# Pairing the last rows of the first two batches in a token-mixing matmul, and moving one transpose and one set of loads

## The chip, the core and the metric

The kernel runs on one core of a Trainium2 chip. The metric is the time of one execution on the device in microseconds (us), the median of several runs; lower is better. The engines are the tensor engine (PE in the profile; PEld is its weight load), the vector engine (DVE), the scalar engine (ACT), GpSimd (POOL) and the sync engine, whose queue (SPq) issues most transfers. PE's results go to PSUM, which this kernel divides into a pool of four single banks ("big") and one of two double banks ("sm").

## The reference, cut to what matters

Eight batches of 576 rows go through linear attention and then through an MLP mixer:

```python
# attention, per batch and head (8 heads of 64 columns)
q_p, k_p = phi(q), phi(k)                   # phi(x) = elu(x) + 1
x = (q_p @ (k_p.T @ v)) / (q_p @ k_p.sum(0) + 1e-6)   # 576 x 512 once the heads are joined
# mixer, per batch
h  = np.maximum(x.T @ w_tok1, 0) @ w_tok2   # mixes the 576 rows, through 256 features
u  = x + h.T
out = u + np.maximum(u @ w_ch1, 0) @ w_ch2  # mixes the 512 columns, through 1536 features
```

576 rows are four blocks of 128 and 64 rows over. The kernel treats two batches as a pair: the 64 last rows of both stand in one tile `ut` of 128 rows (even batch in rows 0 to 63, odd batch in rows 64 to 127). So the transposes and channel matmuls of the last rows are done once per pair.

## The kernel before: the parts that the change and the argument touch

`mm1` and `mm2` are the token matmuls, `mm3` and `mm4` the channel matmuls. `utr` transposes `u` into `uT` for `mm3`, and `utr_tail` transposes `ut` into `uTt`. For pair 0 these transposes are done on PE, later by transfers. `mm2_tails` handles the last rows of both batches together, for pairs 1 to 3 only:

```python
def mm2_tails(p):
    ps = ps_sm.tile([128, 2, DM], FP32, name="h_ps", tag="sm")[:, 0]
    for kt in range(NT):                       # NT = 2
        at = D * (T * kt + 2 * R)
        for b in range(2):                     # both halves of the array, 64 columns each
            nc.tensor.matmul(out=ps[half[b]], lhsT=w2p[:, at:at + D], rhs=ar[b][:, kt, :],
                             start=(kt == 0), stop=(kt == NT - 1))
    for b in range(2):
        h = half[b]
        nc.vector.tensor_tensor(out=ut[p % 2][h], in0=ps[h], in1=x[b][h, R], op=ALU.add)
```

In pair 0, batch 0's last rows are done alone, early, and batch 1's alone, later, with a full-width matmul of which half is thrown away:

```python
def mm2_first_tail():                          # batch 0, between the third and fourth mm3 group
    ps = sm_tile()[:, 0]
    for kt in range(NT):
        nc.tensor.matmul(out=ps[half[0]], lhsT=w2p[:, D * (T * kt + 2 * R):][:, 0:D],
                         rhs=ar[0][:, kt], start=(kt == 0), stop=(kt == NT - 1))
    nc.vector.tensor_tensor(out=ut[0][half[0]], in0=ps[half[0]], in1=x[0][half[0], R], op=ALU.add)

# ... the end of pair 0's first stage, and the start of batch 1's mm3
fill += [(23, fn) for fn in (
    lambda: mm4_end(0, 0), lambda: mm4_end(0, 1), lambda: mm2_half(1, 0),
    lambda: mm4_end(0, 2), lambda: mm2_half(1, 1), lambda: utr(1, [0]),
    lambda: mm2(1, [R]), lambda: utr(1, [1]), lambda: mm4_end(0, 3))]
run(big, sorted(fill, key=lambda e: e[0]))

for mc in range(3):
    mm3(1, mc, range(0, 2))                    # first halves of three groups, three banks of "big"
utr_tail(0)
big = [lambda mc=mc: mm3(1, mc, range(2, 4)) for mc in range(3)] + ...   # (cut)
```

A number such as `(23, fn)` says after which block of the big matmuls a piece is issued. `mm4_end(0, t)` is the DVE add that empties output block t of batch 0 out of its bank. Each engine gets its instructions in the order of the program, and a bank goes to the next user when its last reader is done.

Names in the profile lines below: `c_ps` is the bank of an `mm3` group (four matmuls for 128 of the 1536 features; the first three groups of batch 1 are split into halves of two), `h_ps` that of `mm2` or `mm4`, `tp` that of transposes. "kv" is the block of 72 small matmuls for `k_p.T @ v` of a batch. ACT and DVE share what stands between the matmuls: exp (tile `e`), relu (`cr`, `ar`), copies, and the "v cast", which turns v into bf16 for kv, one half on each of the two engines.

## Time and profile before

| | |
|---|---|
| time, median of 3 runs (range) | 263.65 us (263.41 to 263.68) |
| span in the profile | 261.8 us |
| PE busy; PE's share of the chain that ended last | 96%; 90% |
| DVE busy, ACT busy | 61%, 50% |
| granted PE clock | 1.000 |

PE is almost never idle, so the question for every piece is what it adds to PE's row of instructions or where it makes PE wait. The prediction below shows the lines. Starts in them are in us from the start of the span. A merged line gives the start, the length from the first start to the last end, and the count.

### The profile page before, as it was taken

What the parts mean: (1) busy time and instruction counts of PE and PEld (TensorE: products, weight loads), DVE (VectorE), ACT (ScalarE), POOL (GpSimd) and SP (SyncE); (2) the same over time, 40 slices, a digit from 0 to 9 for tenths busy, and PEclk for the clock granted to TensorE, in tenths of its full rate; (3) what the DMA queues carried; (4) which work ended last, traced back from release to release, by engine and by line L of the source; (5) the groups of instructions that cost most, each with busy time, mean ns of one, the idle gap of its engine ahead of it and who ended that gap; (6) DMA issues with size and microseconds to landing.
All of it is one profiled execution on the core that took longest, in us unless ns stands there. A gap on an engine that the chain in (4) does not pass through costs nothing.

```text
span 261.8 us, 5158 instructions
## 1 busy us (share of the span) xinstructions
PE 252.1 (96%) x2102; PEld 132.2 (50%) x2120; DVE 158.9 (61%) x313; ACT 130.9 (50%) x202; POOL 35.7 (14%) x58
## 2 busy tenths in 40 slices
PE   7799999999999999999999999999999999999993
PEld 3584455555744554455554554455554554444642
DVE  5865969966739687948674377939674263420122
ACT  4755773378374468336780468335780453026300
POOL 9760210110001300030001300030001300000000
PEclk9999999999999999999999999999999999999999
DMA  7999999699307994899999990770066500730043
GB/s 256 249 204 278 370 192 377 240 224 410 119 9 141 201 376 187 124 242 382 322 398 229 303 356 3 168 167 20 3 139 115 120 3 2 154 105 3 0 102 98
DMA packets 50087, 48.34 MB, mean 185 GB/s; under 512 B 30288, under 2 KB 35536, under 8 KB 50064
## 3 DMA queue, kind: packets, MB, share of 16 engines
q1 hardware_dynamic: 41904, 35.53, 46.9%
q0 software_dynamic: 7440, 11.44, 20.8%
q10 hardware_dynamic: 720, 1.05, 1.2%
q8 instruction: 16, 0.26, 0.4%
q14 instruction: 7, 0.06, 0.1%
HBM read 35.85 MB, written 9.44 MB: 173 GB/s over the span
## 4 chain that ended last, share of the span: by engine, by line
PE 90%; DMA 3%; ACT 2%; DVE 1%; POOL 1%; issue 1%; ACTq 0%; POOLq 0%
PE h_ps L529 33%; PE c_ps L503 32%; PE a_ps L248 5%; PE c_ps L517 4%; PE h_ps L261 4%; PE nd_ps L210 3%; DMA cr<-in_v_dram 3%; PE kv_ps L169 2%; PE h_ps L566 1%; PE bank L440 1%; POOL qT L610 1%; PE h_ps L282 1%; PE bank L405 1%; PE bank L378 0%; ACT u L303 0%
## 5 line engine op out<-in xcount | busy, mean ns | idle before, releaser
L503 PE MATMUL c_ps<-uT,wc 128*128 128x512 bf16 x384 | 91.4, 379 | 0.0
L510 ACT ACTIVATE cr<-c_ps 128x512 bf16<-128x512 f32 x91 | 53.4, 599 | 75.6 <-PE c_ps L503 75.5
L529 PE MATMUL h_ps<-wc,cr 128*128 128x512 bf16 x363 | 84.3, 379 | 0.5
L529 PEld LDWEIGHTS <-cr 128*128 128x128 bf16 x372 | 35.6, 98 | 41.7 <-issue 1.2
L503 PEld LDWEIGHTS <-wc 128*128 128x128 bf16 x384 | 35.7, 98 | 36.6 <-issue 1.2
L551 POOL DMA_DIRECT2D out_dram<-o_sb x24 | 14.5, 608 | 150.9 <-DVE o_sb L546 150.7
L546 DVE TENSOR_TENSOR o_sb<-h_ps,u 128x512 f32<-128x512 f32 x31 | 21.0, 687 | 21.0 <-PE h_ps L529 20.9
L222 DVE TENSOR_TENSOR x<-nd_ps,den 128x512 bf16<-128x512 f32 (+1 forms) x42 | 25.3, 602 | 1.4
L139 DVE TENSOR_SCALAR e<-e 128x1152 bf16<-128x1152 bf16 x30 | 14.0, 468 | 15.8 <-ACT e L125 15.7
L125 ACT ACTIVATE e<-q_raw 128x1152 bf16<-128x1152 f32 x16 | 18.5, 1160 | 5.7 <-DMA q_raw<-in_q_dram 5.5
L273 DVE TENSOR_TENSOR u<-h_ps,x 128x1024 bf16<-128x1024 f32 x12 | 14.3, 1219 | 10.1 <-PE h_ps L261 10.1
L125 ACT ACTIVATE e<-k_raw 128x1152 bf16<-128x1152 f32 x16 | 18.7, 1169 | 2.3 <-DMA k_raw<-in_k_dram 2.3
L219 DVE TENSOR_SCALAR den<-nd_ps 128x8 f32<-128x8 f32 (+1 forms) x42 | 6.8, 163 | 17.9 <-PE nd_ps L210 17.2
L210 PEld LDWEIGHTS <-qT 128*128 128x128 bf16 x140 | 11.4, 98 | 9.3 <-issue 0.2
L210 PE MATMUL nd_ps<-kvbd,qT 128*128 128x130 bf16 x140 | 15.1, 223 | 0.0
L248 PE MATMUL a_ps<-x,w 128*128 128x512 bf16 x50 | 13.9, 379 | 0.3
L556 DVE TENSOR_TENSOR o_sb<-h_ps,ut 128x512 f32<-128x512 f32 x4 | 2.8, 689 | 18.7 <-PE h_ps L529 18.7
L151 ACT CAST vs<-v_raw 128x1152 bf16<-128x1152 f32 x12 | 13.9, 1160 | 0.0
L251 ACT ACTIVATE ar<-a_ps 128x512 bf16<-128x512 f32 x14 | 7.6, 594 | 11.4 <-PE a_ps L248 11.4
L261 PE MATMUL h_ps<-ar,w2p 128*128 128x512 bf16 x48 | 12.5, 379 | 0.1
L140 DVE TENSOR_TENSOR qp<-e,y 128x1152 bf16<-128x1152 bf16 x16 | 12.1, 759 | 0.6
L131 DVE TENSOR_SCALAR y<-q_raw 128x1152 bf16<-128x1152 f32 x16 | 12.1, 757 | 0.3
(109 smaller groups left out, 221.3 us busy)
## 6 DMA issues: line engine op xcount, KB each, us to landing
k_raw<-in_k_dram SPq DMA_DIRECT2D x16, 576.0 KB, 9.1
q_raw<-in_q_dram SPq DMA_DIRECT2D x16, 576.0 KB, 7.0
v_raw<-in_v_dram SPq DMA_DIRECT2D x14, 576.0 KB, 10.8
out_dram<-o_sb POOLq DMA_DIRECT2D x24, 256.0 KB, 4.5
wc<-in_moe_w_ch_dram POOLq DMA_DIRECT2D x8, 384.0 KB, 9.5
out_dram<-o_sb SPq DMA_DIRECT2D x9, 128.0 KB, 2.3
out_dram<-o_sb ACTq DMA_DIRECT2D x7, 128.0 KB, 2.6
out_dram<-o_sb POOLq DMA_DIRECT2D x6, 128.0 KB, 7.1
```

The costliest lines, as they stand in the source:

```text
L125: nc.scalar.activation(out=e, in_=f, func=AF.Exp)
L139: nc.vector.tensor_scalar(out=e, in0=e, scalar1=1.0, scalar2=None, op0=ALU.min)
L210: nc.tensor.matmul(out=o[:, a], lhsT=qT[b][:, t0:t0 + 128], rhs=kvbd[b][:, c, a], start=True, stop=True)
L222: nc.vector.tensor_tensor(out=x[b][:, rs[0]:rs[0] + m, HG * D * g:HG * D * (g + 1)].rearrange("p r (h d) -> p r h d", h=HG), in0=v_[:, :, ...
L248: nc.tensor.matmul(out=ps[:, mt], lhsT=w1t[:, b, ms] if r == R else w1[:, r, ms], rhs=x[b][:, r, :], start=(r == 0), stop=(r == R))
L261: nc.tensor.matmul(out=ps[:, i], lhsT=w2v(kt, r, b), rhs=ar[b][:, kt, :], start=(kt == 0), stop=(kt == NT - 1 and not add))
L273: nc.vector.tensor_tensor(out=u[b][:, rs[0]:rs[0] + m], in0=ps[:, 0:m], in1=x[b][:, rs[0]:rs[0] + m], op=ALU.add)
L503: nc.tensor.matmul(out=ps, lhsT=wc1[:, kj, 128 * mc:128 * mc + 128], rhs=uT[b][:, :, kj], start=(kj == 0), stop=(kj == NDM - 1))
L510: nc.scalar.activation(out=cr[b][:, mc, :], in_=ps, func=AF.Relu)
L529: nc.tensor.matmul(out=ps, lhsT=crt[:, kc, :] if t == 8 else cr[b][:, kc, 128 * r:128 * r + 128], rhs=wc2[:, kc, :], start=(kc == 0), stop ...
L546: nc.vector.tensor_tensor(out=o, in0=ps, in1=u[b][:, r, :], op=ALU.add)
L551: (nc.scalar if last and e else put).dma_start(out=outv[2 * p + b, :, 2 * r0 + e:2 * r0 + e + 2 * m - 1:2], in_=live["o"][half[e], 0:m])
```

## The change

Its intent: the last rows of pair 0 are paired like those of the later pairs. Four matmuls in two places become four in one place that run two at a time, which saves time on PE. Their transpose moves behind the fourth matmul group of the next stage (group 3 in the code, which counts from zero), as `ut` is now ready later. The loads of batch 5 go behind pair 1's transpose of the last rows in the transfer queue.

```diff
     def mm2_tails(p):
-        ps = ps_sm.tile([128, 2, DM], FP32, name="h_ps", tag="sm")[:, 0]
+        ps = bank() if p == 0 else ps_sm.tile([128, 2, DM], FP32, name="h_ps", tag="sm")[:, 0]
...
-    def mm2_first_tail():                 # the whole function goes
...
-    fill = [(2, mm2_first_tail)]
+    fill = []
...
-        lambda: mm2(1, [R]), lambda: utr(1, [1]), lambda: mm4_end(0, 3))]
+        lambda: mm2_tails(0), lambda: utr(1, [1]), lambda: mm4_end(0, 3))]
...
     for mc in range(3):
         mm3(1, mc, range(0, 2))
-    utr_tail(0)
...
+    fill += [(3, lambda: utr_tail(0))]
...
             if n == 2:
-                fill += [(12 + d, lambda: load_all(5, "qkv"))]      # d = 1 here
+                fill += [(16, lambda: load_all(5, "qkv"))]          # pair 1's transpose is at 15
```

More of the change, by code (lines that the diff above doesn't have):

```diff
@@ L453, in mm2_first @@
                                 in1=x[0][:, rs[0]:rs[0] + 2, cs], op=ALU.add)
-    def mm2_first_tail():
-        ps = sm_tile()[:, 0]
-        for kt in range(NT):
-            nc.tensor.matmul(out=ps[half[0]], lhsT=w2p[:, D * (T * kt + 2 * R):][:, 0:D],
-                             rhs=ar[0][:, kt],
-                             start=(kt == 0), stop=(kt == NT - 1))
-        nc.vector.tensor_tensor(out=ut[0][half[0]], in0=ps[half[0]], in1=x[0][half[0], R],
-                                op=ALU.add)
     def utr_first(js, put):
```

## The prediction

> **What bounds the kernel now.** I read the page's engine table, its clock strip and the chain of work that ended last first, to see which engine sets the end.
>
> ```profile
> PE 252.1 (96%) x2102; PEld 132.2 (50%) x2120; DVE 158.9 (61%) x313; ACT 130.9 (50%) x202; POOL 35.7 (14%) x58
> ...
> PEclk9999999999999999999999999999999999999999
> ...
> PE 90%; DMA 3%; ACT 2%; DVE 1%; POOL 1%; issue 1%; ACTq 0%; POOLq 0%
> ```
>
> The tensor engine (PE) carries 90% of the chain, at full clock throughout. Only work taken out of its stream, or a gap in it, moves the end; the vector engine (DVE), the scalar engine (ACT) and the transfers count only where PE waits for them. So I went to the timeline of each place that the diff touches. The first is where the last rows of batch 0 are now done alone:
>
> ```profile
> 23.64 1.24 PE L503 MATMUL c_ps<-uT,wc 128*128 128x512 bf16 x5
> 24.81 0.62 PE L458 MATMUL bank<-ar,w2p 128*64 128x512 bf16 x2
> 25.36 0.82 PE L503 MATMUL c_ps<-uT,wc 128*128 128x512 bf16 x3
> ```
>
> Columns: start, length, engine, line, operation. To see here: a 512-column matmul lasts 0.38 us but the next starts 0.216 us after it (a run of 8 such spans 1.73 us in the chain). The last c_ps start is 23.64 + 1.24 - 0.38 = 24.50; the next c_ps is at 25.36. So the two 64-wide matmuls cost 25.36 - 24.50 - 0.216 = 0.64 us, not 2 x 0.216 = 0.43.
>
> The later pairs already use the paired form, four 64-wide matmuls:
>
> ```profile
> 103.99 1.89 PE L529 MATMUL h_ps<-wc,cr 128*128 128x512 bf16 x8
> 105.81 0.62 PE L282 MATMUL h_ps<-ar,w2p 128*64 128x512 bf16 x4
> 106.37 7.08 PE L529 MATMUL h_ps<-wc,cr 128*128 128x512 bf16 x31
> ```
>
> The same sum: 106.37 - (103.99 + 1.89 - 0.38) - 0.216 = 0.65 us for four. The four take what two take: each pair runs side by side.
>
> The third place is the changeover from pair 0's output to batch 1, on PE and then on DVE:
>
> ```profile
> 52.51 0.59 PE L261 MATMUL bank<-ar,w2p 128*128 128x512 bf16 x2
> 52.94 0.61 PE L316 MATMUL tp<-identity,u 128*128 128x128 bf16 x8
> 53.45 1.46 PE L503 MATMUL c_ps<-uT,wc 128*128 128x512 bf16 x6
> 54.74 0.39 PE L481 MATMUL tp<-identity,ut 128*128 128x128 bf16 x4
> 54.96 1.24 PE L503 MATMUL c_ps<-uT,wc 128*128 128x512 bf16 x5
> ```
>
> ```profile
> 52.70 0.69 DVE L320 COPY uT<-tp 128x1024 bf16<-128x1024 bf16 x1 [0.15 <-PE tp L316]
> 53.43 0.69 DVE L269 TENSOR_TENSOR ut<-bank,x 64x512 bf16<-64x512 f32 x1
> 54.15 0.69 DVE L546 TENSOR_TENSOR o_sb<-h_ps,u 128x512 f32<-128x512 f32 x1
> ```
>
> To see: PE is unbroken, and DVE works without a break from 52.70. Three matmul groups (six c_ps records) start between 53.45 and 54.53 while the fourth output block's bank is held until 54.84, when the last of these DVE adds ends. Four banks exist in this pool. So one of the three groups reuses the bank of the last rows. Freed at 53.43 + 0.69 = 54.12, it can only serve the third group, whose two matmuls start at about 54.31 and 54.53. Its slack is thus only about 0.2 us.
>
> The last place is the tail matmul of pair 1, with the wait in the DMA queue:
>
> ```profile
> 127.80 1.03 PE L261 MATMUL h_ps<-ar,w2p 128*128 128x512 bf16 x4
> 128.81 1.05 PE L517 MATMUL c_ps<-uTt,wc 128*128 128x128 bf16 x16
> ```
>
> ```profile
> 111.44 2.32 SPq L112 DMA_DIRECT2D q_raw<-in_q_dram  x2
> 113.85 1.81 SPq L112 DMA_DIRECT2D k_raw<-in_k_dram  x2
> 115.71 1.63 SPq L112 DMA_DIRECT2D v_raw<-in_v_dram  x2
> 117.47 3.62 SPq L492 DMA_TRANSPOSE uTt<-ut  x1
> 121.20 2.62 SPq L112 DMA_DIRECT2D q_raw<-in_q_dram  x2
> ```
>
> The transpose of the last rows stands behind six loads of batch 5 and takes 11.3 us to land (the maximum of its three in the view by tile; the median is 2.8), so at 128.8. Four matmuls from 127.80 should hand over at 128.66; the next starts at 128.81. PE loses 0.15 us there.
>
> **What the Trainium skill says.** "TensorE: Matmul & The Clock Gate", part 3 (The mechanism) says that matmuls on different tiles of the array run concurrently; the pair of 0.65 us above agrees. "TensorEngine Tiling (Array Packing)", Key Properties: "Changing tiling mode (not just tile) drains the TensorE". The trace agrees: 0.64 - 0.43 = 0.21 us is paid for going into the 64-wide form and back. Its section PSUM Bottleneck says that tiling speeds PE but not the emptying of PSUM; the trace agrees, as two 64-row adds (two DVE instructions, 1.39 us at 106.48) follow the paired form, one add of 0.69 us the single form. "DMA: Bandwidth & Descriptors", Issuing engines are not separate DMA queues, says all transfers interleave on 16 engines; moving the loads therefore moves no bytes, only their order.
>
> **The change part by part.**
>
> 1. The two 64-wide matmuls at 24.8 us go: -0.64 us of PE. One DVE add (0.68 us) goes too, in a stretch where DVE is near saturated (it does y, relu, min, max = 0.76 + 0.68 + 0.45 + 0.76 = 2.65 us per three groups, and PE needs 12 x 0.216 = 2.59). From here PE runs 0.64 us earlier, if batch 1's data are there. By the issue times and landing times of the transfers, its q block lands at about 18.54 + 12.0 = 30.5 us and is used at 31.23; 31.23 - 0.64 = 30.6, just enough. The second weight block of the channel output lands at about 36.9 and its matmuls start after the 37.2 to 38.0 kv block: about 0.4 us of room remain. Batch 2's q lands at 43.2 and holds ACT (idle 4.4 us), but ACT then waits 1.9 us more for PE, so nothing is lost. The shift should reach 52 us nearly whole.
> 2. At 52.5 us, two full-width matmuls (0.43 us) become four 64-wide ones (0.65): +0.22. Net PE work of 1 and 2: -0.42 us.
> 3. DVE gets a second add in the changeover: it is busy from 52.70 - 0.64 = 52.06; copy to 52.79, two adds to 52.79 + 1.39 = 54.18. The third group wants that bank at 54.31 - 0.42 = 53.89. It waits 0.33 us (with about 0.05 of handover). Of the 0.42 only 0.09 is left at this point.
> 4. The four transposes of the last rows (0.22 us at 54.74) leave this place and come back unchanged after the fourth matmul group of the stage: -0.22, then +0.22. Their ACT copy (0.59 us) moves from ahead of the relus to behind the fourth. ACT is continuously busy from 55.16 to 62.3, and PE waits about 0.16 us for it in this stretch (30 groups' matmuls take 6.63 us, not 30 x 0.216 = 6.47). The relus that free banks come relatively sooner in the new order, so I credit 0.10 us.
> 5. Loads of batch 5 behind the transpose: it then follows the qT transposes at 111.4 and lands by 115 or so, far ahead of 128.7: -0.15 us. The loads start about 1.5 us later (the other two transposes of this kind took 1.2 to 1.4 us to issue). Batch 5's q landed about 7.6 to 8.2 us after issue, 119 to 121, and is used from 123.1 (DVE) and 123.7 (ACT): no new wait.
>
> Sum: -0.09 (what is left of parts 1 to 3) - 0.10 - 0.15 = -0.34 us, 263.3 us.
>
> **The rivals.**
>
> - *Nothing waits.* The bank choice or DVE's order comes out kindlier; then -0.42 - 0.16 - 0.15 = -0.73, 262.9 us. For it: slack of a few tenths in most places. Against: DVE has no idle slot between 52.70 and 55.5.
> - *The early shift is eaten by transfers.* Batch 1's blocks land at fixed times, and DVE and ACT are fed by them 0.1 to 0.7 us after landing. If 0.3 us is lost there, DVE starts its adds later as well; together with the bank wait the changeover would come out 0.2 us later than before, leaving only the -0.15: 263.5 to 263.7 us. For it: q used at 31.23 just after landing. Against: no DMA wait is listed before ACT or DVE there.
> - *ACT becomes the bound after 55 us.* With the uTt copy behind the fourth relu, the fifth waits 0.59 us more. If PE then stalls for a bank, or kv waits for the v cast, +0.2 to +0.4 us: up to 263.8 us. For it: ACT's unbroken row. Against: the same copy stood before the first relu until now, so the sum of work is the same.
> - *The later loads starve batch 5.* If they land 3 us later, ACT would block with exp at 123.7, and relus behind it: +0.5 us or so. Against: some 2.5 us of room, and the queue is drained soon after either way.
>
> **Range and chances.** The terms lie between -0.75 and +0.3 us. The three runs before span 0.27 us, so a chip's scatter adds 0.1 to 0.15 on either side. Predicted 263.3 us; 8 times in 10 between 262.7 and 263.8. A change of 2% is 5.3 us, seven times the whole gain; only an unforeseen ordering trouble could reach it: faster 0.005, within 2% 0.985, slower 0.01.
>
> **What would show it.** In the changed kernel's timeline: no 64-wide matmuls at 24.8 and four near 52; kv at 37.2 earlier by about 0.6 (part 1). Two 64-row adds back to back on DVE near 52.8, and the third matmul group of batch 1 starting only after them (part 3): if it follows the second without a gap, that step is wrong and the time nearer 262.9. The handover at the next kv block (61.7 before) earlier by only 0.1 to 0.3 (part 4). The uTt transpose landing before 120 and no 0.15 us gap at its first use (part 5). A DMA wait before exp of batch 1 or 5 would speak for the second or fourth rival; a time above 264 us would mean that a term is missing.

## The result, and the profile after

| | before | changed |
|---|---|---|
| median of 4 runs | 263.66 us (263.41 to 263.92) | 263.41 us (263.19 to 264.26) |
| span in the profile | 261.8 us | 261.7 us |

The ratio is 0.9996, 95% interval 0.9972 to 1.002. Ratios here are the mean time of one kernel's fast runs over that of the other's fast runs of the same rounds, so not quite the ratio of the medians quoted. By the time alone the change cannot be told from nothing: one run of the changed kernel was 264.26 at a granted clock of 0.993. The trace can resolve more, because its steps agree between runs to a few hundredths of a microsecond.

One correction comes first. The start of the first large matmul depends on a load (v of batch 0) and differs from run to run: 21.50 in the trace of before, 21.76 in this one, and from 20.99 to 22.05 over all traces, whatever the kernel. I therefore count stretches from event to event and not from the span's start.

The changed kernel's PE rows from the first mm3 matmul to the first kv block, the stretch in which the two lone 64-wide matmuls stood:

```profile
21.76 1.02 PE L494 MATMUL c_ps<-uT,wc 128*128 128x512 bf16 x4
22.62 0.61 PE L460 MATMUL tp<-identity,u 128*128 128x128 bf16 x8
23.06 9.84 PE L494 MATMUL c_ps<-uT,wc 128*128 128x512 bf16 x44
...
36.79 0.78 PE L169 MATMUL kv_ps<-vs,kp 64*64 64x65 bf16 x72
```

The 44 matmuls from 23.06 now stand in one line, with no other matmul among them. The ends of the same stretch in the kernel before:

```profile
21.50 1.02 PE L503 MATMUL c_ps<-uT,wc 128*128 128x512 bf16 x4
...
37.19 0.78 PE L169 MATMUL kv_ps<-vs,kp 64*64 64x65 bf16 x72
```

From 21.76 to kv at 36.79 it is 15.03 us; before it was 37.19 - 21.50 = 15.69. So 0.66 us came out, where 0.64 had been forecast.

The changeover to batch 1, PE and then DVE, the counterpart of the lines from 52.51 on in the prediction:

```profile
52.19 0.62 PE L282 MATMUL bank<-ar,w2p 128*64 128x512 bf16 x4
52.75 0.62 PE L316 MATMUL tp<-identity,u 128*128 128x128 bf16 x8
53.21 3.89 PE L494 MATMUL c_ps<-uT,wc 128*128 128x512 bf16 x16
56.93 0.39 PE L472 MATMUL tp<-identity,ut 128*128 128x128 bf16 x4
57.15 4.48 PE L494 MATMUL c_ps<-uT,wc 128*128 128x512 bf16 x20
61.63 0.78 PE L169 MATMUL kv_ps<-vs,kp 64*64 64x65 bf16 x72
```

```profile
52.30 0.69 DVE L320 COPY uT<-tp 128x1024 bf16<-128x1024 bf16 x1 [0.15 <-PE tp L316]
52.91 1.38 DVE L286 TENSOR_TENSOR ut<-bank,x 64x512 bf16<-64x512 f32 x2
54.32 0.69 DVE L537 TENSOR_TENSOR o_sb<-h_ps,u 128x512 f32<-128x512 f32 x1
```

How to read a stall out of a merged line: 16 matmuls without a gap span 15 x 0.216 + 0.38 = 3.62 us, and the line says 3.89. So 0.27 us of waiting is inside it. The 20 matmuls from 57.15 span 19 x 0.216 + 0.38 = 4.48, so there is none. (The 44 above would span 9.67 and take 9.84: a wait of 0.17 us, which the kernel before has too, in the eight matmuls ahead of the lone ones.) In the chain of work that ended last, the piece that goes from DVE to PE names the place:

```profile
52.30 0.60 DVE uT L320
52.91 0.67 DVE ut L286
53.59 0.71 DVE ut L286
54.34 1.04 PE c_ps L494 x4
```

The two adds end at 52.91 + 1.38 = 54.29 and the third group starts at 54.34. Those two adds have become part of the chain; before, PE had no DVE step here. Behind the third group the chain leaves PE once more and runs over relu, exp and a v cast on ACT and DVE to the next kv block. What that costs is small and comes up under end_first_tail6.

From the transposes of batch 1's u (52.06 before, 51.66 now) to kv of batch 2 (61.68 before, 61.63 now) it was 9.62 us and is 9.97. Of the 0.66 us won, 0.35 is given back in this stretch. The lines of before:

```profile
52.06 0.61 PE L316 MATMUL tp<-identity,u 128*128 128x128 bf16 x8 [0.24 <-ACT u L303]
...
54.96 6.79 PE L503 MATMUL c_ps<-uT,wc 128*128 128x512 bf16 x30
61.68 0.78 PE L169 MATMUL kv_ps<-vs,kp 64*64 64x65 bf16 x72
```

The transfer queue and the first use of pair 1's `uTt`:

```profile
107.12 4.10 SPq L199 DMA_TRANSPOSE qT<-qp  x2
111.31 3.05 SPq L483 DMA_TRANSPOSE uTt<-ut  x1
114.46 1.05 SPq L112 DMA_DIRECT2D q_raw<-in_q_dram  x2
...
119.19 1.53 SPq L112 DMA_DIRECT2D q_raw<-in_q_dram  x2
```

```profile
127.84 1.03 PE L261 MATMUL h_ps<-ar,w2p 128*128 128x512 bf16 x4
128.70 1.06 PE L508 MATMUL c_ps<-uTt,wc 128*128 128x128 bf16 x16
```

The transpose is issued 6 us earlier. Its first use follows the four matmuls after 128.70 - 127.84 = 0.86 us = 4 x 0.216: no gap. Before it was 128.81 - 127.80 = 1.01.

### The profile page after: what moved, and what is told of

It reads as the page before. It is cut to its first block, busy times and chain, and to the rows that moved or that the text cites. A ratio compares the mean times of both kernels' runs of the same rounds, so it can differ in the third digit from the quotient of the medians.

```text
span 261.7 us, 5173 instructions
## 1 busy us (share of the span) xinstructions
PE 252.2 (96%) x2120; PEld 132.1 (50%) x2120; DVE 159.0 (61%) x313; ACT 130.7 (50%) x202; POOL 35.9 (14%) x58
## 4 chain that ended last, share of the span: by engine, by line
PE 88%; DVE 3%; DMA 3%; ACT 3%; POOL 1%; issue 1%; ACTq 0%; POOLq 0%
PE h_ps L520 33%; PE c_ps L494 29%; PE a_ps L248 6%; PE c_ps L508 4%; PE h_ps L261 4%; PE nd_ps L210 3%; DMA cr<-in_v_dram 3%; PE kv_ps L169 2%; PE h_ps L557 1%; PE bank L440 1%; ACT e L125 1%; POOL qT L601 1%; PE h_ps L282 1%; DVE kp L140 1%; DVE ut L286 1%
## 5 line engine op out<-in xcount | busy, mean ns | idle before, releaser
L251 ACT ACTIVATE ar<-a_ps 128x512 bf16<-128x512 f32 x14 | 7.6, 595 | 10.7 <-PE a_ps L248 10.7
```

## The experiments

All kernels gave correct results. One run of before, at 297.54 us and a clock of 0.853, is left out of the ratios.

Four stretches of the trace carry the reading. They are differences of two start times on PE:

* **A**: first mm3 matmul to kv of batch 1 (the lone matmuls stood here);
* **B**: transposes of batch 1's u to kv of batch 2 (the changeover);
* **C**: kv of batch 4 to the first matmul on pair 1's `uTt`;
* **tail**: the start of that matmul from the span's start.

| kernel | A | B | C | tail | median | before, same rounds | ratio (95%) |
|---|---|---|---|---|---|---|---|
| before (trace) | 15.69 | 9.62 | 14.57 | 128.81 | | | |
| changed: run change | 15.03 | 9.98 | 14.42 | 128.62 | 263.15 | 263.93 | 0.9974 (0.9946 to 1.0002) |
| changed: change_again | 15.03 | 9.97 | 14.42 | 128.36 | 263.42 | 263.64 | 0.9987 (0.9954 to 1.002) |
| loads_only | 15.69 | 9.62 | 14.42 | 128.68 | 263.81 | 263.93 | 1.0 (0.9973 to 1.0026) |
| pairs_only | 15.03 | 9.98 | 14.91 | 128.85 | 264.02 | 263.93 | 1.0 (0.998 to 1.002) |
| end_first | 15.04 | 9.70 | 14.48 | 128.15 | 262.99 | 263.93 | 0.9962 (0.9941 to 0.9982) |
| end_first_again | 15.16 | 9.71 | 14.41 | 127.72 | 262.92 | 263.64 | 0.9962 (0.9927 to 0.9997) |
| end_first_loads_back | 15.03 | 9.71 | 14.86 | 128.89 | 263.26 | 263.64 | 0.9982 (0.9945 to 1.0018) |
| end_first_tail6 | 15.27 | 9.63 | 14.42 | 127.75 | 262.91 | 263.95 | 0.9966 (0.9939 to 0.9993) |
| tail6_again | 15.03 | 9.63 | 14.54 | 127.89 | 263.10 | 263.64 | 0.9968 (0.9936 to 0.9999) |
| third_add | 15.15 | 10.71 | 14.42 | 129.22 | 264.01 | 263.95 | 1.0001 (0.9976 to 1.0026) |
| tail_old_place | 15.03 | 10.05 | 14.53 | 129.10 | 263.60 | 263.95 | 0.9987 (0.996 to 1.0014) |

C varies by about 0.1 us between traces even where nothing in it was touched (the first changed trace has 14.51), so only the 0.4 to 0.5 us steps in it and the gap at its end are used.

My theory: the matmuls come out as computed, and the third group of batch 1 then waits for DVE's second add, because it takes the bank of the last rows. The rivals: transfers that arrive at fixed times eat the gain in A; or ACT's row bounds the stretch B.

### change and change_again: the changed kernel once more

No edit.

> The changed kernel again, unaltered, to see its traced steps on another execution and its time beside the others of these rounds. Theory (the third matmul group of batch 1 waits for two vector adds): its start stands about 0.3 us late against an unbroken row of the groups before it, and the time is 0.1 to 0.5 us under the kernel before. Rival (the early gain is lost to transfers): no gap ahead of the third group, and the stretch from the first c_ps matmul to the kv block at 37 us is not shorter than before. The start of the first kv matmuls at 11 us is set by a load and may differ by 0.3 us from run to run in any kernel.

> The changed kernel once more, in the same rounds as the two reordered ones. Between 0.2 and 0.5 us under the kernel before by the traced steps; single runs spread by over 1 us, so the rounds may not resolve it.

A is shorter by 0.66 us in both, and the 0.27 us gap is in both: each has the 16 matmuls in 3.89 us. change_again is the cleanest pair with the trace of before, as both have their first mm3 matmul at 21.50. Its span is 261.3 us against 261.8, and the last block of matmuls starts at 254.63 against 255.09: 0.46 us earlier. That is 0.66 - 0.35 + 0.15. The times point the same way (ratios 0.9974 and 0.9987), but both intervals hold 1.

### loads_only: the loads of batch 5 alone

```diff
 # in the kernel before
             if n == 2:
-                fill += [(12 + d, lambda: load_all(5, "qkv"))]
+                fill += [(16, lambda: load_all(5, "qkv"))]
```

> The kernel before with only the loads of batch 5 moved behind the transpose of the last rows. If the parts are independent, everything up to 105 us is as before, the transpose lands before 120 us in place of 128.8, and the tail matmuls at 128.8 follow the four before them without the gap of 0.15 us: the time falls by 0.15 us. Rival (this wait was hidden behind something else): the gap goes and a later block, the uT transposes at 131 or the kv block at 146, loses the same 0.15 us again: 0.

A and B are exactly those of before; the transpose is issued at 111.61 and lands 5.3 us later; C falls by 0.15 us. At the next kv block (batch 5) the gain is still there: 146.13 against 146.26. So the first reading holds: the wait was exposed, and taking it away is worth 0.13 to 0.15 us. The time cannot show so little.

### pairs_only: the change without moving the loads

```diff
 # in the changed kernel
             if n == 2:
-                fill += [(16, lambda: load_all(5, "qkv"))]
+                fill += [(12 + d, lambda: load_all(5, "qkv"))]
```

> The changed kernel with the loads of batch 5 put back ahead of the transpose. The gap of 0.15 us at the first tail matmuls of pair 1 is back, the transpose lands near 128 us; the time lies 0.15 us over the changed kernel and within 0.3 us of the kernel before: -0.05 to -0.3. If the wait of the third group takes the place of the matmuls removed, the kv block of batch 2 (61.7 us before) starts, counted from the first c_ps matmul, 0.3 us earlier than before and not 0.64.

The kv of batch 2 came 0.30 us earlier relative to the first mm3 matmul, as expected. But the gap was not 0.15 us. This is PE at the first use of `uTt` in this run:

```profile
127.50 1.03 PE L261 MATMUL h_ps<-ar,w2p 128*128 128x512 bf16 x4
128.85 1.05 PE L508 MATMUL c_ps<-uTt,wc 128*128 128x128 bf16 x16 [0.33 <-DMA uTt<-ut]
```

The four matmuls would hand over at 127.50 + 0.86 = 128.36, and the next starts at 128.85: 0.49 us. The transpose is issued at 117.55, takes 11.3 us, and its first use starts at 128.85 as it did at 128.81 before, although PE was there 0.30 us earlier. So the whole gain of the pairing was lost again at one wait. My expectation of a time 0.05 to 0.3 us under the kernel before was wrong: by the trace it is 0.04 us later at this matmul, and the ratio is 1.0. The two parts of the change don't add up. Alone they give nothing (pairing) and 0.13 to 0.15 (loads), together 0.45.

### end_first: the bank of the third group freed earlier

```diff
         lambda: mm4_end(0, 2), lambda: mm2_half(1, 1), lambda: utr(1, [0]),
-        lambda: mm2_tails(0), lambda: utr(1, [1]), lambda: mm4_end(0, 3))]
+        lambda: mm4_end(0, 3), lambda: mm2_tails(0), lambda: utr(1, [1]))]
```

No work is added or removed. PE's row of instructions is the same; on DVE one output add goes ahead of the two adds to `ut`.

> The changed kernel with one reordering: the output add of the fourth block is issued ahead of the last rows' matmuls and their two adds, so that the third matmul group of batch 1 gets the fourth block's bank and not the last rows'. Theory (bank wait): the third group follows the second without a gap, the kv block of batch 2 comes 0.2 to 0.3 us earlier than in the changed kernel, and the time falls by about 0.25 us under it. Rival (the scalar engine's row or the v cast bounds this stretch): the gap of the third group goes, but kv does not start earlier: 0. Rival (transfers): nothing changes.

PE and DVE in this run:

```profile
52.96 3.62 PE L494 MATMUL c_ps<-uT,wc 128*128 128x512 bf16 x16
...
61.11 0.78 PE L169 MATMUL kv_ps<-vs,kp 64*64 64x65 bf16 x72
```

```profile
52.05 0.69 DVE L320 COPY uT<-tp 128x1024 bf16<-128x1024 bf16 x1 [0.15 <-PE tp L316]
52.66 0.68 DVE L537 TENSOR_TENSOR o_sb<-h_ps,u 128x512 f32<-128x512 f32 x1
53.26 1.38 DVE L286 TENSOR_TENSOR ut<-bank,x 64x512 bf16<-64x512 f32 x2
```

Sixteen matmuls now take 3.62 us, the value without a gap. The two adds end later than in the changed kernel's order (53.26 + 1.38 = 54.64), and it costs nothing, because the bank they read is not the one the third group takes. B falls from 9.98 to 9.70: 0.28 us, all of the gap. This speaks for the bank wait and against ACT or the v cast as the bound in this stretch. The kernel is 262.99 us against 263.93 of before, ratio 0.9962 (0.9941 to 0.9982). This interval lies below 1; the difference to the changed kernel itself is within the scatter.

### third_add: the suspected wait in a larger dose

```diff
-        for b in range(2):
+        for b in ((0, 1, 1) if p == 0 else (0, 1)):
             h = half[b]
             nc.vector.tensor_tensor(out=ut[p % 2][h], in0=ps[h], in1=x[b][h, R], op=ALU.add)
```

> The changed kernel with the second add of pair 0's last rows done twice (same result). A dose of the suspected wait: the vector engine frees the bank one add later. Theory: the third group starts 0.7 us later than in the changed kernel, kv of batch 2 0.6 to 0.7 us later, and the kernel comes 0.6 us over the changed one, so 0.1 to 0.3 over the kernel before. Rival (slack hides the adds): the third group and kv stay where they are.

PE around the third group, and DVE's adds:

```profile
53.07 1.03 PE L494 MATMUL c_ps<-uT,wc 128*128 128x512 bf16 x4
54.94 2.75 PE L494 MATMUL c_ps<-uT,wc 128*128 128x512 bf16 x12 [0.84 <-DVE ut L286]
```

```profile
52.78 2.11 DVE L286 TENSOR_TENSOR ut<-bank,x 64x512 bf16<-64x512 f32 x3
```

The two groups ahead would hand over at 53.07 + 4 x 0.216 = 53.93; the third starts at 54.94, just after 52.78 + 2.11 = 54.89. The gap is 1.01 us in place of 0.27: one add of 0.7 us more on DVE, 0.74 us more wait on PE. B grows by 0.73, and all of it stays to the end of the span: the last block of matmuls starts at 255.49, 0.86 us behind change_again, of which 0.12 is a load wait in A (see end_first_tail6). That is 0.40 us behind the kernel before, a little over the 0.1 to 0.3 I had expected. The median is 264.01 against 263.95 of before: the dose has used up the gain, as the first reading asked.

### tail_old_place: the transpose of the last rows where it was

```diff
     for mc in range(3):
         mm3(1, mc, range(0, 2))
+    utr_tail(0)
...
-    fill += [(3, lambda: utr_tail(0))]
```

> The changed kernel with the transposes of pair 0's last rows back ahead of the second halves of the first three groups. The third group already waits for the adds that these transposes need, so they add no wait of their own; the copy returns ahead of the relus. My step says that this move by itself is worth 0.0 to 0.1 us: kv of batch 2 within 0.1 us of the changed kernel. If the move was needed to hide the second add, kv comes 0.3 us or more later.

B is 10.05 against 9.98: moving the transposes is worth 0.07 us in this kernel. The third group already waits until both adds are done, so the transposes behind it find their input ready. It was not the move that hid the second add. What the move does remove is a small wait further on: with the transposes back in their old place, the 30 matmuls behind them take 6.78 us, as in the kernel before (6.79), where 29 x 0.216 + 0.38 = 6.64 would be without a gap.

### end_first_tail6 and tail6_again: the copy of the last rows behind the v cast

```diff
 # in end_first
-    fill += [(3, lambda: utr_tail(0))]
+    fill += [(6, lambda: utr_tail(0))]
```

> The reordered kernel of the run end_first, and besides the transposes of the last rows behind the seventh matmul group of the stage in place of the fourth, so that their copy on the scalar engine comes after the v cast. In end_first the kv block of batch 2 still starts 0.16 us after the last group before it could hand over; the v cast on the scalar engine ends 0.05 us before kv starts. If kv waits for that cast, kv now follows without a gap: 0.16 us less than end_first, 0.7 us less than the kernel before by the traced steps. Rival (kv waits for the other v cast, on the vector engine, or for a bank): no gain over end_first.

> The reordered kernel with the last rows' transposes at the seventh group once more: 0.07 us less than end_first by the traced steps (kv follows the transposes of batch 1 by 9.63 us), so no difference from it that the times can show. Where its first c_ps matmul is early, exp of batch 1 waits for its q block and the start is not all kept.

The copy on ACT now comes after the v cast, which ends at 59.11 + 1.18 = 60.29, well ahead of kv at 60.76:

```profile
58.94 1.89 PE L494 MATMUL c_ps<-uT,wc 128*128 128x512 bf16 x8
60.76 0.78 PE L169 MATMUL kv_ps<-vs,kp 64*64 64x65 bf16 x72
```

```profile
59.11 1.18 ACT L151 CAST vs<-v_raw 128x1152 bf16<-128x1152 f32 x1
60.15 0.64 ACT L501 ACTIVATE cr<-c_ps 128x512 bf16<-128x512 f32 x1
60.64 0.62 ACT L474 COPY uTt<-tp 128x512 bf16<-128x512 bf16 x1
```

B falls by 0.07 us only, not by 0.16. The eighth matmul starts at 58.94 + 1.89 - 0.38 = 60.45 and would hand over at 60.66; kv starts at 60.76. So 0.10 us of what I had taken for a wait for the cast is still there without it. About the same, 24.81 - 24.50 - 0.216 = 0.09, stands before the 64-wide matmuls in the kernel before. I read it as the cost of leaving the full-width form. The wait for the cast was the other 0.06 to 0.07: in end_first, ACT's cast ends at 59.87 + 1.19 = 61.06 and kv starts at 61.11; in the changed kernel it is 61.58 and 61.63.

This pair also showed the rival of the transfers at work. In end_first_tail6 the first mm3 matmul was early, at 20.99. This is ACT at the exp of batch 1's q in that run:

```profile
29.58 0.60 ACT L501 ACTIVATE cr<-c_ps 128x512 bf16<-128x512 f32 x1 [0.27 <-PE c_ps L494]
30.61 1.16 ACT L125 ACTIVATE e<-q_raw 128x1152 bf16<-128x1152 f32 x1 [0.43 <-DMA q_raw<-in_q_dram]
```

ACT waits 0.43 us for the q block; A is 15.27 and not 15.03. third_add (0.32 us of wait, A 15.15) and end_first_again (0.3 us, A 15.16) show it too. In the runs with A = 15.03 or 15.04 the exp starts at most 0.2 us late, and that much costs nothing. So the shift of 0.66 us has taken up the room that this load had: where PE starts early or the load is late, 0.1 to 0.25 us of the gain is lost here.

The median of end_first_tail6 and end_first cannot be told apart: ratios 0.9966 and 0.9968 against 0.9962 and 0.9962. Both beat the kernel before in every set of rounds they were in, by 0.3 to 0.4%.

### end_first_loads_back: the larger gain against the same landing

```diff
 # in end_first
             if n == 2:
-                fill += [(16, lambda: load_all(5, "qkv"))]
+                fill += [(12 + d, lambda: load_all(5, "qkv"))]
```

> The reordered kernel of end_first with the loads of batch 5 put back ahead of the transpose of the last rows. In pairs_only the transpose landed at 128.8 us whatever the tensor engine had gained, and the whole gain of 0.30 us was lost there. If that landing is the bound, this kernel loses its larger gain of 0.57 us at the same place too: the wait at the first tail matmul of pair 1 grows to about 0.7 us, that matmul starts at 128.7 to 128.9 us after the span's start, and the time equals that of the kernel before within 0.1 us. Rival (the loads are issued earlier with the rest and the transpose lands earlier too): the first tail matmul comes 0.3 us or more before 128.8 and the kernel keeps part of the gain.

The first use of `uTt` starts at 128.89. So it is 128.81, 128.85 and 128.89 us in the three kernels with the loads ahead, whatever PE had gained, and each keeps nothing of its gain by this point. The expectation about the landing held. The size of the wait did not: it is 128.89 - (127.59 + 0.86) = 0.44 us, not 0.7, because this run had lost 0.36 us earlier, in a wait of another kind. This is PE at the first mm4 block behind kv of batch 1:

```profile
36.53 0.78 PE L169 MATMUL kv_ps<-vs,kp 64*64 64x65 bf16 x72
37.67 1.02 PE L520 MATMUL h_ps<-wc,cr 128*128 128x512 bf16 x4 [0.36 <-DMA wc<-in_moe_w_ch_dram]
```

It waits for the second block of w_ch2, which comes behind batch 1's q block. None of the other traces shows it. The median of the times, 263.26 against 263.64, ratio 0.9982 (0.9945 to 1.0018), has an interval that holds both no gain and the whole of end_first's (0.9962). The expected equality within 0.1 us is neither shown nor refuted by it.

### loads_swapped: how much room the later loads have

```diff
             if n == 2:
-                fill += [(16, lambda: load_all(5, "qkv"))]
...
             fill += [(18, lambda: load_all(n + 4, "qkv"))]
+            if n == 2:
+                fill += [(18, lambda: load_all(5, "qkv"))]
```

> The changed kernel with the loads of batch 5 issued after those of batch 6, to see how much room the move left. The q of batch 5 then lands near 128 us, over 4 us after its first use; exp on the scalar engine waits for it with relus behind it, and the tensor engine stalls 3 to 6 us: 266 to 269 us. If the scalar engine's queue has more room than the trace suggests, the time stays within 1 us of the changed kernel.

One look, at 270.85 us and a granted clock of 0.985 (a single run, so its state is unknown; the 0.985 may be a consequence of the wait or add to the time). ACT and PE in it:

```profile
130.18 1.16 ACT L125 ACTIVATE e<-q_raw 128x1152 bf16<-128x1152 f32 x1 [6.38 <-DMA q_raw<-in_q_dram]
```

```profile
132.37 1.93 PE L261 MATMUL h_ps<-ar,w2p 128*128 128x512 bf16 x4 [4.45 <-ACT ar L251]
```

The exp waits 6.38 us for q of batch 5, relus stand behind it, and PE stops for 4.45 us. After it the four matmuls take 1.93 us in place of 1.03. So the loads can be too late as well as too early: behind the transpose is right, behind batch 6 cost some 7 us in this run. The wait was in the range I gave (3 to 6 us on PE), the time was over the range (266 to 269). What I had left out is the stretch after the wait: the matmuls from 132.37 to 137.50 take 5.13 us, and the same ones take 2.62 in the changed kernel (127.84 to 130.46). With the 4.45 of the wait, these 2.5 us make up the 7.

## Why the prediction was right, and where its steps were off

The measured 263.41 us lies in the range 262.7 to 263.8 and beside the predicted 263.3. That alone says little: the range also holds the 263.66 of the kernel before, and with single runs 1 us apart a median so close is in part luck. The mechanism can be judged by the trace. It held in parts 1 to 4, with sizes that were partly off; part 5 was right only as it stood beside the others:

* **Part 1** (-0.64): -0.66 in A in the traces with no load wait. The second rival, transfers, was given as possible at the q block of batch 1: it does show in some executions, with 0.1 to 0.25 us, and in one at the w_ch2 block, for which I had estimated 0.4 us of room.
* **Part 2** (+0.22): from the transposes of batch 1's u to the first mm3 matmul it was 53.45 - 52.06 = 1.39 and is 53.21 - 51.66 = 1.55 us, so +0.16.
* **Part 3** (a wait of 0.33 us): 0.27. end_first removed it, third_add made it 0.74 us larger, and in both the end moved with it. This cause is shown.
* **Part 4** (-0.10): the 0.16 us of bank wait in this stretch of the kernel before is indeed gone (20 matmuls in 4.48 us, no gap), and kv waits 0.07 us for the v cast in its place: together -0.09. tail_old_place, which undoes the move alone, gives 0.07. The third rival, ACT as the bound, is right for these 0.07 us and not for more.
* **Sum of 1 to 4**: predicted -0.19 at kv of batch 2; by the terms measured -0.66 + 0.16 + 0.27 - 0.09 = -0.32, in the trace -0.30 or -0.31. The difference from the prediction comes from the first three terms, each 0.02 to 0.06 us off in the same direction.
* **Part 5** (-0.15): right by itself, loads_only shows 0.15. What the step lacked was that it does not stand apart from the others. I had written it as one more term of a sum. The landing of the transpose is a fixed point that the pairing alone would have run into, so moving the loads was worth 0.13 to 0.15 us before the pairing and 0.49 after it (first use at 128.85 in pairs_only, 128.36 in change_again). The sum came out right only because both parts were in the change. Two of its smaller numbers were off: the transpose took 3.05 us to issue, so the loads start 3.0 us later (111.44 before, 114.46 now) and not 1.5, and it lands at 116.5 and not by 115.
* **The fourth rival** (later loads starve batch 5) named just such a delay of 3 us, and still it did not come: q of batch 5 lands 5.6 to 6.4 us after its issue, where it took 7.6 to 8.2 before, and its exp starts at 123.78 us without a wait, as at 123.74 before. loads_swapped shows that it would come with a longer delay.

The sum in the trace is -0.45 us, where -0.34 was predicted; the medians differ by 0.25 in the rounds of the result, by 0.78 and 0.22 in those of change and change_again. Single runs spread over about 1 us, so the time agrees with the trace without adding to it.

The rival "nothing waits" (262.9 us) is what end_first realises: with one output add issued ahead of the pair's adds, the changeover has no gap, and the medians were 262.99 and 262.92.

## What to carry to other kernels

When a matmul is packed tighter, follow what reads its PSUM bank: the pairing halved PE's time for these matmuls but doubled the vector adds that free the bank, and the next group that took this bank paid for it; the cure was an order of release, not less work. Where an engine is the bound, look for points that arrive at fixed times (a transfer behind large loads) further on in its row, because time saved ahead of such a point is worth nothing until the point is moved, and then the two gains come together. With effects of 0.1 to 0.5 us in 264, let stretches between two events of the trace decide and use the timed rounds as a check only.

## What the Trainium skill lacked or had wrong

* "TensorE: Matmul & The Clock Gate", Back-to-back issue gap, gives about 131 ns per matmul as sustained for 512 columns, and about 216 ns as the gap of single ones. Every gapless row here has 216 ns between starts (16 in 3.62 us, 20 in 4.48 us, 36 in 7.94 us); nothing near 131 was seen. Part 2 of the same page has 215.7 ns as measured back to back, which agrees.
* "TensorEngine Tiling (Array Packing)", Key Properties, says that a change of tiling mode drains the engine but gives no size. Here about 0.1 us stands before the first 64-wide matmul, and 0.64 - 0.43 = 0.21 us is paid for going in and coming back.
* "DMA: Bandwidth & Descriptors" has no figure for a small transfer behind large ones in the same queue. Here the transpose of a 128 x 512 tile took 10.7 to 11.3 us to land behind six loads of 576 KB and 5.2 to 6.1 us ahead of them.
